# DeltaNet recurrence and SwiGLU FFN in one kernel: products of the preparation placed in the same TensorE visits as the recurrence's

## The chip, the cores and the metric

The kernel runs on one core of one Trainium2 chip. The metric is device time of one execution in microseconds (us), as the median of repeated runs. TensorE does the matrix products, VectorE and ScalarE the elementwise work, GpSimd a few small operations, and SyncE (SP in the profile) issues nearly all transfers.

## The reference

Attention of the DeltaNet kind over 4 batches, 8 heads, 768 positions and a head size of 48, and then a feed-forward block over the 3072 tokens (model size 384, inner size 1536). Everything is float32.

```python
k_n = k / (np.linalg.norm(k, axis=-1, keepdims=True) + 1e-06)
state = np.zeros((B, H, D, D))
for t in range(S):
    kt, vt, bt = k_n[:, :, t], v[:, :, t], beta[:, :, t, None]
    y[:, :, t] = np.einsum('bhd,bhde->bhe', q[:, :, t], state)
    v_old = np.einsum('bhde,bhd->bhe', state, kt)
    state = state + bt[:, :, :, None] * np.einsum('bhd,bhe->bhde', kt, vt - v_old)
x = y.transpose(0, 2, 1, 3).reshape(B * S, H * D)
g = x @ w_gate
out = (g * (1 / (1 + np.exp(-g))) * (x @ w_val)) @ w_out
```

## The kernel before

**Chunks.** The sequence is cut into 12 chunks of 64 positions. Inside a chunk the recurrence is turned into matrix products; between chunks only `state` is handed on. Chunk c's attention ends in x, and the FFN of chunk c works on it (256 tokens). While TensorE works on the FFN of chunk c, the small products of the attention of chunk c + 1 are put between its large ones. The order of the instructions of all engines is written out by hand: what the Python code issues first stands first in its engine's queue (`manual_schedule`).

**The FFN of a chunk** is six calls of `gate_val` (lines 840 to 868) and one output. Each `gate_val` makes a group of six matmuls for `p_gate` and six for `p_val`; the page counts two records to a matmul, so such a group is "x12". ScalarE takes silu into `sil` (one buffer), VectorE multiplies into `h_f`. From chunk 3 on the output is `output_fast` (line 950): seven products of six matmuls each (`p_o`, line 959, "x84" in all), with sums of `h_f` on VectorE beforehand (lines 942 to 948) and additions into `o_sb` (line 969) as products end.

**The attention of a chunk** on TensorE is made of batches of 32 products of 64x64 tiles, for which the text uses short names:

- R (`p_r`, line 742): K times state; VectorE scales `vin` by the norms (line 401) and subtracts R from it (line 759)
- Y1 (`p_y`, line 751): Q times state
- U (`p_u`, line 763): the inverse `zt` times `vin`; ScalarE copies it to `uu`
- S (`p_s`, line 794): K transposed times `uu`; VectorE adds it to `state` (line 803)
- Y2 (`p_y`, line 782): the masked K Q^T times `uu`, accumulated on Y1; ScalarE copies the sum to `y`
- F (`p_f`, line 827): six full transposes of `y`; ScalarE copies them to `x_ffn`, which the next FFN reads

They are the steps of the generator `advance` (line 730): R and Y1, then U, then S and Y2, then F.

**The preparation** that comes ahead of a chunk's attention:

- K and Q are transposed in blocks by VectorE out of `qpad` (line 422, 128x1024 each, in `turned`), which then starts the load of the next blocks on SP (line 154, eight transfers for K and eight for Q)
- K K^T (`gram`, line 444, copied to `a_sb` by line 467) and K Q^T (line 444, masked into `p_sb` by VectorE, line 459); both are batches of 32 products of 64x64 tiles
- for each pair of chunks, an inverse on VectorE (`invert`, line 641): transposes of `a_sb` into `mb` (lines 477, 480), GpSimd's power (line 655), scaling, 31 steps of two operations each (`substitute`, lines 510 and 516), and transposes into `zt` and `z1`. Its pieces are issued by `fill(n)`, which `gate_val` and the output call between their own work
- for each pair of chunks, two joins, J1 (line 706) and J2 (line 720), each 64 products of 32x32 tiles: J1 reads `a_sb` and `zt`, ScalarE scales the result to `t2`, J2 multiplies by `z1`, and ScalarE and then VectorE copy the result into `zt`

**PSUM.** The eight banks are split by hand: a pair `px`, a pair `py`, and four banks that the FFN's tiles take in turn. R, U, S, K K^T and J1 use `px`; Y1 with Y2, F, K Q^T and J2 use `py`. A pair is taken again only when its last reader is done.

**Where small products stand.** `point(c)` is called ahead of every `gate_val` and between output products. Each call issues one step of `advance(c)` if one has begun, else one piece of preparation (`prep_step`: a join, the second half of K and Q products that have been transposed, or new transposes). A stretch of small products between two large groups is called a visit here.

Of the kernel before, what the change touches and what calls it, by code (L numbers as in the profile page):

```python
# [11 lines left out]
ALU = mybir.AluOpType  # L12
# [9 lines left out]
def kernel(  # L22
# [25 lines left out]
    nc = tc.nc  # L48
# [21 lines left out]
    def ps_pair(name, tag):  # L70

        return psum.tile([128, 2, 512], FP32, name=name, tag=tag, bufs=1)

    def ps_ffn(shape, name):
        return psum.tile(shape, FP32, name=name, tag="ffn", bufs=4)
# [261 lines left out]
    def every():  # L337
        for bp in range(NB):
            for j in range(NJ):
                for n, (par, b) in enumerate(ORDER):  # L340
                    yield bp, j, par, b, bp == 0 and j == 0
# [128 lines left out]
    def gram(*args):  # L470
        for _ in gram_steps(*args):
            pass
# [100 lines left out]
    def recur(p, m=D):  # L573
        p = p[:, :, 0 : NB * NJ * m]
        return p.rearrange("p x (bp j d) -> p x bp j d", bp=NB, j=NJ)
# [120 lines left out]
    def join(g):  # L696

        zt, a, z1 = ztp[g % ZB], a_sb[g], z1s[g]
        M = HH // 2
        p_j = ps_pair("p_j", "px")[:, 0].rearrange("p (c m i) -> p c m i", c=2, m=M)  # L700
        for c in range(2):
            for m in range(M):
                for e in range(2):
                    for s in range(2):
                        dst, lo = QUADS[2 * s + e][0], QUADS[2 * s + 1][0]
                        nc.tensor.matmul(
                            p_j[dst, c, m],
                            a[lo, c, 2 * m + e, 0:R],
                            zt[lo, c, 2 * m + e, R:C],
                        )  # L710
        t2 = work.tile([128, 2, M, R], FP32, name="t2", tag="tmp", bufs=1)
        nc.scalar.mul(t2, p_j, -1.0)
        yield
        p_j = ps_pair("p_j", "py").rearrange("p e (c m i) -> p e c m i", c=2, m=M)
        for c in range(2):
            for m in range(M):
                for e in range(2):
                    for s in range(2):
                        row, hi = QUADS[2 * s + e][0], QUADS[2 * s][0]
                        nc.tensor.matmul(p_j[hi, e, c, m], z1[row, c, m], t2[row, c, m])  # L720
        zt_v = zt.rearrange("p c (m e) i -> p e c m i", e=2)
        for s, copy in ((0, nc.scalar.copy), (1, nc.vector.tensor_copy)):
            hi = QUADS[2 * s][0]
            copy(
                zt_v[hi, :, :, :, R:C].rearrange("p e c m i -> p e (c m) i"),
                p_j[hi].rearrange("p e c m i -> p e (c m) i"),
            )
        yield

    def advance(c):  # L730

        kn = knp[slot(c)]
        zt = ztp[c // 2 % ZB][:, c % 2]
        zt = zt.rearrange("p (par bp j) i -> p par bp j i", par=2, bp=NB)
        if c > 0:
            scale_v(c)
        r = vin.pop(c)
        p_y = recur(ps_pair("p_y", "py"))
        if c > 0:
            p_r = recur(ps_pair("p_r", "px"))  # L740
            for bp, j, par, b, first in every():
                nc.tensor.matmul(  # L742
                    p_r[half_of(b ^ par), par, bp, j],
                    kt[c][half_of(par), bp, j, b],
                    state[half_of(par), b, bp, j],
                    start=first,
                    stop=True,
                    skip_group_check=True,
                )
            for bp, j, par, b, first in every():  # L750
                nc.tensor.matmul(  # L751
                    p_y[half_of(b ^ par), par, bp, j],
                    qt[c][half_of(par), bp, j, b],
                    state[half_of(par), b, bp, j],
                    start=first,
                    stop=False,
                    skip_group_check=True,
                )
            nc.vector.tensor_tensor(out=r, in0=r, in1=p_r, op=ALU.subtract)  # L759
        yield  # L760
        p_u = recur(ps_pair("p_u", "px"))
        for bp, j, par, b, first in every():
            nc.tensor.matmul(  # L763
                p_u[half_of(b), par, bp, j],
                zt[half_of(b ^ par), par, bp, j],
                r[half_of(b ^ par), par, bp, j],
                start=first,
                stop=True,
                skip_group_check=True,
            )  # L770
        uu = work.tile([128, 2, NB, NJ, D], FP32, name="uu", tag="r", bufs=2)
        each = range(NB) if c == 0 else (slice(0, NB),)
        for bp in each:
            nc.scalar.copy(uu[:, :, bp], p_u[:, :, bp])
        if c + 2 < NCH:
            load_v(c + 2)
        yield
        pq = p_sb.pop(c)

        def p_of_u():  # L780
            for bp, j, par, b, first in every():
                nc.tensor.matmul(  # L782
                    p_y[half_of(b ^ par), par, bp, j],
                    pq[half_of(b), par, bp, j],
                    uu[half_of(b), par, bp, j],
                    start=(c == 0 and first),
                    stop=True,
                    skip_group_check=True,
                )

        def of_state():
            p_s = recur(ps_pair("p_s", "px"))
            for bp, j, par, b, first in every():
                nc.tensor.matmul(  # L794
                    p_s[half_of(par), b, bp, j],
                    kn[half_of(b), bp, 2 * j + par],
                    uu[half_of(b), par, bp, j],
                    start=first,
                    stop=True,
                    skip_group_check=True,  # L800
                )
            if c > 0:
                nc.vector.tensor_tensor(out=state, in0=state, in1=p_s, op=ALU.add)
            else:
                nc.scalar.copy(state, p_s)
            for later in range(AHEAD, NCH):
                if freed_by_k(later) == c:
                    load_k(later)

        if 0 < c < NCH - 1:  # L810
            of_state()
        p_of_u()
        y = work.tile([128, NB, NJ, 2, D], FP32, name="y", tag="r", bufs=2)
        for bp in each:
            nc.scalar.copy(y[:, bp, :, 0], p_y[:, 0, bp])
            for b in range(2):
                nc.scalar.copy(y[half_of(b), bp, :, 1], p_y[half_of(1 - b), 1, bp])
        yield

        y_f = y.rearrange("p bp j par d -> p bp (j par d)")  # L820
        xts[c] = ffn_pool.tile([128, KT, TOK], FP32, name="x_ffn")
        p_f = ps_pair("p_f", "py")[:, :, 0 : KT * 128]
        p_f = p_f.rearrange("p bp (t n) -> p t bp n", t=KT)
        for bp in range(NB):
            for t in range(KT):
                at = slice(t * 128, (t + 1) * 128)
                nc.tensor.transpose(p_f[:, t, bp], y_f[:, bp, at], ident)
        x_v = xts[c].rearrange("p t (bp n) -> p t bp n", bp=NB)
        for bp in each:
            nc.scalar.copy(x_v[:, :, bp], p_f[:, :, bp])  # L830
        yield
        if c == 0:
            of_state()
            yield
# [181 lines left out]
    def step(kind, fn, *args):  # L1016
        key = (kind, args or (1,))
        if key not in gens:
            gens[key] = [fn(*args), 0]
        next(gens[key][0], None)  # L1020
        gens[key][1] += 1

    def steps(kind, *args):
        return gens.get((kind, args), (None, 0))[1]

    fills = []
# [32 lines left out]
    def may_advance(c):  # L1059
        g = c // 2  # L1060
        due = {0: 1, 1: 2 + 2 * (c % 2)}.get(g, 2)
        return steps("advance", c) > 0 or (c in p_sb and steps("join", g) >= due)

    def prep_step(c):
# [23 lines left out]
        going.append(gen)  # L1088
        return True

    def point(c):

        mine = c < NCH and steps("advance", c) < 4 and may_advance(c)
        if mine and steps("advance", c) > 0:
            step("advance", advance, c)
        elif not prep_step(c - 1) and mine:
            step("advance", advance, c)

    def finish(c):

        if c < NCH:
            while not may_advance(c):
                fill_some(1000)
                prep_step(c - 1)
            while steps("advance", c) < 4:
                step("advance", advance, c)
# [190 lines left out]
```

## Time and profile before

| | |
|---|---|
| median of 8 runs | 738.26 us (738.1 to 739.06) |
| the profiled execution, its own time | 738.1 us |
| its span in the trace | 736.4 us |
| TensorE busy | 697.9 us, 95% of the span |
| TensorE weight loads, beside the products | 605.5 us |
| VectorE busy | 473.0 us, 64% |
| ScalarE, GpSimd busy | 154.6 us, 67.1 us |

Busy time is the time in which an engine had an instruction at work. The FFN of chunk 3 begins at 250.4 us after the span's start, that of chunk 4 at 306.4, of chunk 5 at 361.4, of chunk 6 at 417.5, and the last product ends at about 732 us. In the lines of the timeline the first number is the start in us from the span's start, the second the duration in us; a number in brackets is the idle time ahead of it and what ended it. Lines of the waits give the total in us, how often, and the longest.

### The profile page before, as it was taken

Reading aid. Unit: us, or ns where it says so; the run is one execution under the profiler, and the core shown is the slowest. Engines: PE = TensorE matmul, PEld = TensorE weight load, DVE = VectorE, ACT = ScalarE, POOL = GpSimd, SP = SyncE. Lnnn points to the kernel's source line nnn. Section 1 sums busy time; section 2 is a strip of 40 time slices with the busy share of each in tenths; the row PEclk is TensorE's granted clock in tenths of the full one; section 3 lists DMA queues with packets and bytes.
Section 4 is the critical chain, followed back from the end, with each engine's and each line's share of the span. In section 5 each row is a group of like instructions: output and inputs, shape, how many; then the busy total and the mean of one; then the engine's idle time right before and its main releaser. Section 6 shows DMA issues by size and latency. Waiting matters only on the chain.

```text
span 736.4 us, 22478 instructions
## 1 busy us (share of the span) xinstructions
PE 697.9 (95%) x10132; PEld 605.5 (82%) x10132; DVE 473.0 (64%) x977; ACT 154.6 (21%) x287; POOL 67.1 (9%) x46
## 2 busy tenths in 40 slices
PE   4657899999999999999999999999999999999997
PEld 3545788866787788988988988988988988989987
DVE  6999988888498163678853678854678853313122
ACT  3555443302401112021012011012011012021010
POOL 7008100202100000030000030000030000000000
PEclk9556999999999999999999999999999999999999
DMA  7775444221231112331302231302211100100000
GB/s 147 178 235 148 115 110 127 42 35 24 57 45 24 23 24 45 47 64 16 50 3 46 39 68 22 50 3 42 47 25 14 31 3 3 23 3 0 22 1 21
DMA packets 130735, 37.18 MB, mean 50 GB/s; under 512 B 122864, under 2 KB 125936, under 8 KB 130640
## 3 DMA queue, kind: packets, MB, share of 16 engines
q1 hardware_dynamic: 127184, 34.01, 22.7%
q10 hardware_dynamic: 3072, 1.57, 1.0%
q8 instruction: 79, 1.29, 0.7%
q0 software_dynamic: 384, 0.17, 0.2%
q14 instruction: 16, 0.13, 0.1%
HBM read 31.01 MB, written 4.72 MB: 49 GB/s over the span
## 4 chain that ended last, share of the span: by engine, by line
PE 80%; DVE 16%; issue 1%; POOL 1%; DMA 1%; ACT 0%; ACTq 0%; DVEq 0%; SPq 0%
PE p_gate L847 23%; PE p_val L847 23%; PE p_o L959 15%; PE p_o L876 6%; DVE tmp L510 3%; DVE zb L516 3%; PE p_g L444 2%; PE p_u L763 2%; PE p_r L742 1%; PE p_s L794 1%; PE p_y L782 1%; PE p_y L751 1%; POOL n_t L365 1%; DVE h_f L917 1%; DVE last_h L287 1%
## 5 line engine op out<-in xcount | busy, mean ns | idle before, releaser
L847 PE MATMUL p_gate<-x_ffn,wg_sb 128*128 128x256 f32 x864 | 204.9, 387 | 1.4 <-ACT x_ffn L830 1.4
L847 PE MATMUL p_val<-x_ffn,wv_sb 128*128 128x256 f32 x864 | 198.6, 380 | 0.0
L847 PEld LDWEIGHTS p_val<-x_ffn,wv_sb 128*128 128x128 f32 x864 | 164.1, 190 | 22.0
L847 PEld LDWEIGHTS p_gate<-x_ffn,wg_sb 128*128 128x128 f32 x864 | 161.6, 192 | 24.1 <-ACT x_ffn L830 1.9
L862 DVE TENSOR_TENSOR h_f<-sil,p_val 128x512 f32<-128x512 f32 x71 | 48.5, 683 | 147.5 <-PE p_val L847 147.1
L856 ACT ACTIVATE sil<-p_gate 128x512 f32<-128x512 f32 x72 | 43.0, 598 | 277.1 <-PE p_gate L847 249.4
L655 POOL TENSOR_TENSOR n_b<-mb,half 128x32 f32<-128x32 f32 x5 | 43.3, 8661 | 408.0 <-DVE mb L480 368.2
L959 PE MATMUL p_o<-wo_sb,h_f 128*128 128x192 f32 x432 | 75.6, 329 | 0.1
L959 PEld LDWEIGHTS p_o<-wo_sb,h_f 128*128 128x128 f32 x432 | 70.3, 190 | 1.2 <-DVE o_sb L969 0.7
L510 DVE TENSOR_TENSOR tmp<-zb,mb 128x31 f32<-128x31 f32 (+15 forms) x186 | 63.3, 340 | 12.1 <-PE p_j L630 6.8
L516 DVE TENSOR_TENSOR zb<-zb,tmp 128x31 f32<-128x31 f32 (+15 forms) x186 | 63.8, 343 | 6.6 <-DVE tmp L510 0.2
L969 DVE TENSOR_TENSOR o_sb<-o_sb,p_o 128x192 f32<-128x192 f32 x45 | 15.8, 350 | 53.4 <-PE p_o L959 36.2
L876 PE MATMUL p_o<-wo_sb,h_f 128*128 128x384 f32 x136 | 45.7, 490 | 0.0
L876 PEld LDWEIGHTS p_o<-wo_sb,h_f 128*128 128x128 f32 x136 | 25.4, 190 | 16.4
L959 PE MATMUL p_o<-last_k,h_f 128*128 128x192 f32 x180 | 32.2, 326 | 0.0
L959 PEld LDWEIGHTS p_o<-last_k,h_f 128*128 128x128 f32 x180 | 29.8, 190 | 0.0
L917 DVE TENSOR_TENSOR h_f<-h_f,h_f 128x256 f32<-128x256 f32 x54 | 22.4, 424 | 8.0 <-PE p_o L959 7.1
L959 PE MATMUL p_o<-last_h,h_f 128*128 128x192 f32 x144 | 26.3, 326 | 0.0
L959 PEld LDWEIGHTS p_o<-last_h,h_f 128*128 128x128 f32 x144 | 23.9, 190 | 0.0
L254 ACT ACTIVATE last_h<-last_h,rebias 128x512 int32<-128x512 uint32 (+2 forms) x26 | 15.3, 616 | 30.4 <-DVE last_h L246 30.4
L763 PEld LDWEIGHTS p_u<-vin,zt 64*64 64x64 f32 x768 | 13.7, 141 | 6.9 <-issue 3.2
L763 PE MATMUL p_u<-vin,zt 64*64 64x48 f32 x768 | 15.7, 228 | 2.4 <-DVE vin L759 1.2
(180 smaller groups left out, 691.6 us busy)
## 6 DMA issues: line engine op xcount, KB each, us to landing
vin<-in_v_dram SPq DMA_DIRECT2D x96, 48.0 KB
kn<-in_k_dram SPq DMA_DIRECT2D x40, 96.0 KB
out_dram<-o_sb SPq DMA_DIRECT2D x36, 96.0 KB
zt<-in_moe_w_out_dram SPq DMA_DIRECT2D x6, 384.0 KB
staged<-in_moe_w_out_dram SPq DMA_DIRECT2D x6, 384.0 KB
qpad<-in_q_dram SPq DMA_DIRECT2D x36, 64.0 KB
wo_sb<-in_moe_w_gate_dram SPq DMA_DIRECT2D x4, 512.0 KB
wo_sb<-in_moe_w_val_dram SPq DMA_DIRECT2D x4, 512.0 KB
```

The costliest lines, as they stand in the source:

```text
L254: nc.scalar.activation(power.bitcast(I32), power, ACTF.Relu, bias=rebias, scale=8.0)
L510: nc.vector.tensor_tensor(out=t_v, in0=zb[:, 0 : j + 1, j : j + 1].to_broadcast([128, j + 1, m]), in1=mb[:, j : j + 1, j + 1 : R].to_broad ...
L516: nc.vector.tensor_tensor(out=zb[:, 0 : j + 1, j + 1 : R], in0=zb[:, 0 : j + 1, j + 1 : R], in1=t_v, op=ALU.add,)
L655: nc.gpsimd.tensor_tensor(out=n, in0=mb.rearrange("p j i -> p (j i)")[:, 0 : R * R : R + 1], in1=half, op=ALU.pow,)
L763: nc.tensor.matmul(p_u[half_of(b), par, bp, j], zt[half_of(b ^ par), par, bp, j], r[half_of(b ^ par), par, bp, j], start=first, stop=True, ...
L847: nc.tensor.matmul(ps[name][:, i], w_sb[:, t, (f + i) * 128 : (f + i + 1) * 128], xts[c][:, t], start=(t == 0), stop=(t == KT - 1),)
L856: nc.scalar.activation(sil, ps[name], ACTF.Silu)
L862: nc.vector.tensor_tensor(out=hs[c, f], in0=sil, in1=ps["p_val"], op=ALU.mult)
L876: nc.tensor.matmul(p_o, hs[c, f - f % 2][:, f % 2, bp * 128 : (bp + 1) * 128], wo_sb[:, f], start=(f == 0), stop=(f == FT - 1),)
L917: nc.vector.tensor_tensor(out=out, in0=a, in1=b, op=ALU.subtract)
L959: nc.tensor.matmul(p[x, part], a(f - f % 2)[:, f % 2], b(f), start=not begun and f == 0, stop=f == FH - 1, skip_group_check=True,)
L969: nc.vector.tensor_tensor(out=out, in0=a, in1=b, op=ALU.add)
```

## The change

`advance` is cut anew for every chunk: R and its subtraction are a step, and Y1 goes to U's step. From the FFN of chunk 3 on (c > 3), `point` calls a new function `merged(c)`, which goes through fixed stages: 0, K's and Q's transposes on VectorE at the chunk's start; 1, R with K Q^T and, for even c, J1 (not until the pair's inverse has been issued); 2, J2 for even c, with K K^T of a later chunk; 3, Y1 with U; 4, S with Y2; 5, F. K Q^T moves from the chunk before to the chunk that uses it, K K^T from about the end of one FFN to the second or third visit of the next. The first join takes one of the FFN's four banks instead of `px`.

The order of TensorE's instructions, by FFN; g is a group of gate, v of val, o the output's products (o18 is 18 matmuls), square brackets are visits. J1, J2 in the FFN of chunk 2 before belong to the join of the first form.

```
FFN  before
 2   g v [J2] g v g v [KK+KQ] g v [R+Y1] g v [U] g v [S+Y2] o [F] o [J1]
 3   g v [J2] g v g v [KQ] g v [R+Y1] g v [U] g v [S+Y2] o18 [F] o24 [KK+KQ]
 4   g v [R+Y1] g v [U] g v [S+Y2] g v [F] g v g v [KK+KQ] o42      (6 the same)
 5   g v g v [J1] g v [J2] g v [R+Y1] g v [U] g v [S+Y2] o18 [F] o24 [KK+KQ]   (7 the same)
 8   g v [R+Y1] g v [U] g v [S+Y2] g v [F] g v g v [KQ] o42
 9   as 5, with [KQ] at the end
10   g v [R+Y1] g v [U] g v [Y2] g v [F] g v g v o42
FFN  after
 2   g v [J2] g v g v [KK+KQ] g v [R] g v [Y1+U] g v [S+Y2] o [F] o
 3   g v [R+KQ+J1] g v [J2] g v [Y1+U] g v [S+Y2] g v [F] g v o42
 4   g v [R+KQ] g v [KK] g v [Y1+U] g v [S+Y2] g v [F] g v o42      (6, 8 the same)
 5   g v g v g v g v [R+KQ+J1] g v [J2+KK] g v [Y1+U] o18 [S+Y2] o12 [F] o12   (7 the same)
 9   as 5, with [J2] alone
10   g v [R+KQ] g v [Y1+U] g v [Y2] g v [F] g v g v o42
```

The diff:

```diff
@@ join
-        p_j = ps_pair("p_j", "px")[:, 0].rearrange("p (c m i) -> p c m i", c=2, m=M)
+        p_j = ps_ffn([128, 512], "p_j").rearrange("p (c m i) -> p c m i", c=2, m=M)
@@ advance
         r = vin.pop(c)
-        p_y = recur(ps_pair("p_y", "py"))
         if c > 0:
             p_r = recur(ps_pair("p_r", "px"))
             for bp, j, par, b, first in every():
...
+            nc.vector.tensor_tensor(out=r, in0=r, in1=p_r, op=ALU.subtract)
+        yield
+        p_y = recur(ps_pair("p_y", "py"))
+        if c > 0:
             for bp, j, par, b, first in every():
                 nc.tensor.matmul(
                     p_y[half_of(b ^ par), par, bp, j],
...
-            nc.vector.tensor_tensor(out=r, in0=r, in1=p_r, op=ALU.subtract)
-        yield
         p_u = recur(ps_pair("p_u", "px"))
@@ ahead of point
+    stage_of = {}
+
+    def merged(c):
+        if c >= NCH:
+            return
+        at, k_c, q_c = stage_of.get(c, (0, None, None))
+        g = c // 2
+
+        def a_step():
+            step("advance", advance, c)
+
+        def gram_k(tag):
+            if k_c is not None:
+                gram(k_c, False, tag, (nc.vector.tensor_copy,) * 2)
+                if k_c % 2 == 1:
+                    fills.append((k_c // 2, invert(k_c // 2)))
+
+        def j_step():
+            if c % 2 == 0 and steps("join", g) < 2:
+                step("join", join, g)
+
+        if at == 0:
+            if going:
+                next(going.pop())
+                return
+            if k_of and steps("advance", freed_by_k(k_of[0])) >= 4:
+                k_c = k_of.pop(0)
+                turned(k_c, False)
+            if q_of and q_of[0] == c:
+                q_c = q_of.pop(0)
+                turned(q_c, True)
+        elif at == 1:
+            if c % 2 == 0 and g not in inverted:
+                return
+            a_step()
+            if q_c is not None:
+                gram(q_c, True, "py")
+            if c % 2 == 0:
+                j_step()
+            elif k_c is None:
+                at = 2
+        elif at == 2:
+            if c % 2 == 0:
+                j_step()
+            gram_k("px")
+        elif at < 6:
+            a_step()
+        stage_of[c] = (at + 1, k_c, q_c)
+
     def point(c):
+        if c > 3:
+            merged(c)
+            return
@@ finish
-        if c < NCH:
+        if c > 3:
+            while c < NCH and steps("advance", c) < 4:
+                if stage_of.get(c, (0,))[0] == 1 and c % 2 == 0 and c // 2 not in inverted:
+                    fill_some(1000)
+                merged(c)
+        elif c < NCH:
```

## The prediction

> **What bounds the kernel now.** I read the engine shares first, then the slices with the clock row, then TensorE's waits, then its timeline.
>
> ```profile
> PE 697.9 (95%) x10132; PEld 605.5 (82%) x10132; DVE 473.0 (64%) x977; ACT 154.6 (21%) x287; POOL 67.1 (9%) x46
> PE   4657899999999999999999999999999999999997
> DVE  6999988888498163678853678854678853313122
> PEclk9556999999999999999999999999999999999999
> ```
>
> TensorE is full from the seventh slice on, at full clock, so what the change touches (FFN 3 on, from 250 us) is a TensorE queue: only shorter TensorE work or fewer TensorE waits count there. From 230 us on TensorE waits for just two things:
>
> ```profile
> PE p_g L444 <- DVE kt L422: 1.9, 2, 0.9
> PE p_g L444 <- DVE qt L422: 1.0, 1, 1.0
> ```
>
> The timeline of TensorE (start us, duration us) prices a visit of small matmuls. First stretch: FFN 5. Second: the only place where 64x64 tiles are followed at once by 32x32 ones. Third: a wait, in FFN 6.
>
> ```profile
> 382.39 2.75 PE L847 MATMUL p_val<-x_ffn,wv_sb 128*128 128x256 f32 x12
> 385.08 1.15 PE L742 MATMUL p_r<-state,kt 64*64 64x48 f32 x64
> 386.04 1.11 PE L751 MATMUL p_y<-state,qt 64*64 64x48 f32 x64
> 387.09 2.86 PE L847 MATMUL p_gate<-x_ffn,wg_sb 128*128 128x256 f32 x12
> 389.78 2.75 PE L847 MATMUL p_val<-x_ffn,wv_sb 128*128 128x256 f32 x12
> 392.46 1.15 PE L763 MATMUL p_u<-vin,zt 64*64 64x48 f32 x64
> 393.54 2.86 PE L847 MATMUL p_gate<-x_ffn,wg_sb 128*128 128x256 f32 x12
> 396.24 2.75 PE L847 MATMUL p_val<-x_ffn,wv_sb 128*128 128x256 f32 x12
> ...
> 67.49 1.15 PE L794 MATMUL p_s<-uu,kn 64*64 64x48 f32 x64
> 68.57 0.75 PE L620 MATMUL p_j<-zt,a_sb 32*32 32x32 f32 x64
> ...
> 452.41 2.75 PE L847 MATMUL p_val<-x_ffn,wv_sb 128*128 128x256 f32 x12
> 456.11 1.16 PE L444 MATMUL p_g<-kt 64*64 64x64 f32 x64 [0.95 <-DVE kt L422]
> 457.33 1.16 PE L444 MATMUL p_g<-qt,kt 64*64 64x64 f32 x64
> 458.42 2.22 PE L959 MATMUL p_o<-wo_sb,h_f 128*128 128x192 f32 x12
> ```
>
> Durations overlap, so I use start to start. Without a visit beside it, a gate or val group takes 2.59 (447.23 to 449.82). From 389.78 to 396.24 two groups and a lone U take 6.46: U costs 6.46 - 5.18 = **1.28**. From 382.39 to 389.78, with R and Y1: 7.39 - 5.18 = **2.21**. So a second product costs 0.93 and the visit itself **0.35**, as delays of about 0.10 before it, 0.12 at its end and 0.10 in the group after it. A lone join (375.80 to 379.70 and on) costs 1.41, so its product is 1.06. F, in full 128x128 tiles, leaves its neighbours at 2.59: it is no visit in this sense.
>
> The wait: val of 452.41 ends at 455.00, the next group starts at 458.42; 3.42 where two products take 2.0. VectorE's timeline shows why:
>
> ```profile
> 454.44 0.43 DVE L516 TENSOR_TENSOR zb<-zb,tmp 128x256 f32<-128x256 f32 x1
> 454.81 1.25 DVE L422 STREAM_TRANSPOSE kt<-qpad 128x1024 f32<-128x1024 f32 x1
> 455.98 1.20 DVE L422 STREAM_TRANSPOSE qt<-qpad 128x1024 f32<-128x1024 f32 x1
> ```
>
> The transposes of K and Q stand behind substitution steps of the inverse, and TensorE is asked for K K^T immediately after them.
>
> [...] S to J1 above takes 1.08 where S to Y2 takes 0.96 (398.92 to 399.89), so 0.12 is seen. [...]
>
> **The change, part by part.** The orders of instructions say what moves; the number of matmuls does not change.
>
> *Visits.* From FFN 2 on there are 45 visits before and 36 after (F left out): FFN 2 six to five; FFN 3, 5, 7 and 9 six to four; FFN 4, 6 and 8 four and four; FFN 10 three and three. By chunk, with the products that come or go: FFN 2 loses J1 as a visit of its own, -1.41; FFN 3 loses two visits, K K^T and one K Q^T and gains J1, -0.70 - 1.86 + 1.06 = -1.50; FFN 5, 7 and 9 lose two visits each, -0.70; FFN 8 gains K K^T, +0.93; FFN 10 gains K Q^T, +0.93. Together **-3.15**, which is nine visits at 0.35.
> Against it stand six changes of mode inside visits: J1 behind K Q^T in FFN 3, 5, 7, 9, and K K^T behind J2 in FFN 5 and 7. Each is at least the 0.12 seen and at most 0.22 (0.12 and another 0.10, as a group after a visit shows). I take 0.17: **+1.0**. Ends: 0.7 to 1.3, and 0 if nothing of it adds.
>
> *The waits that go.* By the prices, FFN 4 would take 6 x 5.18 + 3 x 2.21 + 1.28 + 0.65 (F) + 13.65 (42 output matmuls) = 53.3; it takes 306.41 to 361.44 = 55.0. FFN 6: 417.46 to 472.48, the same. FFN 8 (K Q^T alone: 52.4) takes 528.50 to 582.08 = 53.6. The differences are 1.7, 1.7 and 1.2: **-4.6**. They are VectorE's lateness at K K^T, and 0.2 more at the last output product in FFN 4 and 6. After, both transposes are issued at the chunk's start, when VectorE has only the last o_sb add before them: they run from 0.5 to 2.9 us, and K Q^T is asked for at 6.2. That cover is 3.3 us; K K^T comes 7 us later still.
>
> *The wait that is new.* R's subtract, K Q^T's mask and the inverse now meet in FFN 5, 7 and 9. Every step, with row durations: K K^T in FFN 4 is at 12.6 to 13.7 us. VectorE: copies to a_sb to 15.1; three transposes of 2.14 and one product to 22.1; GpSimd's power 6.2 to 28.4 (POOL n_b, L655); norms, beta and scaling of mb, 3.57 as at 432.43 to 436.00, to 32.1 (behind h_f and its sums). 31 steps of two operations follow, 0.45 to 0.92 each, 23.3 together; 15 are done when FFN 4 ends. In FFN 5, from its start: 0.5 (last o_sb add), seven steps 6.3, the transposes of K and Q 2.3, two steps 1.6, h_f 0.6, five steps 3.3, h_f 0.6, two steps 1.0: 16.1. Then zt's transposes 5.8 as at 365.47 to 371.27: **21.8**. J1 stands behind R and K Q^T, four pairs in: 20.7 + 2.0 = 22.7, so 0.9 to spare. Then h_f 0.6, z1 2.4, h_f with sums 1.9, vin scaling 1.05, subtract 0.9, mask 1.25: **29.8**. Bank pair py is held by K Q^T until then, and J2 writes py: it is asked for at 20.7 + 3.4 + 5.2 = 29.4. With the handover of 0.1, TensorE waits **0.5**; FFN 7 is the same. In FFN 9 there is no K to transpose, all is 1.2 earlier, no wait. Sum **+1.0**; ends 0 and 4 (each sum of some 40 durations may be off by 1.5). What is queued behind J2 is all of TensorE.
>
> *Costed at nothing.* Y1 moves to U's visit: its products are in the sum; py is taken later, and U's operand vin is ready then, since a group lies between R and it. (At 89.37 U waited 1.22 for vin; VectorE sets that time, with Y1 before it or not.) The first join's bank in the four-bank FFN ring: v3 must be freed before gate 5; h_f frees it at 22.4, gate 5 starts at 24.1: 1.7 to spare, and if that cover goes, each us late is a us. ScalarE (21%) keeps all its copies; F follows Y2 by 3.9 us of output products where y's three copies take 1.44, and x_ffn's 0.8 has 3.9 behind F. SP: the sixteen loads of K and Q blocks (4 to 6 us of issue for each eight) go behind the output's four instead of ahead of them; they land for a transpose some 50 us later, where the shortest interval before was 43. v's and kn's loads move with U and S by up to 10 us, for a use over 50 us on. GpSimd: the same seven operations a pair of chunks, alone.
>
> **Sum.** 738.1 (profiled; its span is 736.4 and 1.7 lies around it; the median is 738.26, 0.02% off) - 3.15 + 1.0 - 4.6 + 1.0 = **732.3**.
>
> **Rivals.** (1) *The waits move along*: K Q^T now waits for qt at its new place. For: VectorE runs behind in even chunks. Against: no inverse is running at the start of FFN 4, 6 and 8. Only the visits count: 738.1 - 2.1 = 736.0.
> (2) *VectorE becomes the bound in FFN 5, 7 and 9*, and the kernel is **slower**: the inverse starts 14 us later in FFN 4 than before (K K^T was ahead of its first gate), so zt, subtract and mask come late. With an added lateness of L the waits are 2(0.5 + L) + (L - 0.8). They eat the 6.75 of gains at L = 2.2, and cost over 0.2% from L = 2.7. At L = 4 the time is 743.5. Before, FFN 5 shows VectorE just as late: h_f at 371.27 belongs to a val that ended 5 us earlier. Against: my sum leaves 0.5.
> (3) *Between them*, L = 1 to 1.5: 735.3.
> (4) *It does not merge*: the order shows that it does; nothing is left for this.
>
> **Numbers.** Chances: forecast 0.70, (1) 0.09, (3) 0.08, L around 2.2 and so no change 0.06, (2) 0.07. About 0.2% (1.5 us) can be told from no change. Some of (1) falls within it: faster 0.83, same 0.09, slower 0.08. Range: 738.1 - 3.15 - 4.6 = 730.3 with no new cost; upward to (1) and (3), 736.3.
>
> **What would show it.** FFN 4, 6 and 8 at 53.3 us each with no wait at L444; FFN 5 and 7 near 56.2; the transposes of K and Q within 3 us of the chunk's start; zt's end at 21.8 and the mask's at 29.8 in FFN 5; a wait of some 0.5 us of J2 for p_sb. Wrong: waits of over 2 us at J1 or J2 (rival 2), a wait of K Q^T for qt (rival 1), or visits that cost as much when merged.

## The result, and the profile after

The kernel after the change takes **742.27 us** as a median of 11 runs (741.76 to 747.15), the one before 738.65 us in 31 runs taken with it: ratio 1.0065, 95% interval 1.0055 to 1.0076. It is slower, where 732.3 us and faster was forecast. The profiled execution of after takes 746.21 us, with a span of 744.5, so it is one of the longer ones; the section on the prediction says how the two stand to each other.

The engine shares and the clock row of the page of after, to be laid beside those of before:

```profile
PE 702.8 (94%) x10132; PEld 611.1 (82%) x10132; DVE 472.4 (63%) x977; ACT 154.4 (21%) x287; POOL 64.1 (9%) x46
...
PEclk9556999999999999999999999999999999999999
```

The number of TensorE records is the same, but they take 702.8 us in place of 697.9, and more idle time lies between them. The clock row shows nothing of it: a loss of 3 us does not show in a slice of 18.6. TensorE's waits from 230 us on name it (total, times, longest, in us):

```profile
PE p_j L706 <- issue: 5.4, 4, 1.6
```

No wait for kt or qt is left, and none of J2 for `p_sb`. In their place the first join stands still four times, with nothing in another engine that it waits for ("issue"). TensorE's timeline in FFN 3, at the merged visit:

```profile
256.10 1.15 PE L741 MATMUL p_r<-state,kt 64*64 64x48 f32 x64
257.06 1.13 PE L444 MATMUL p_g<-qt,kt 64*64 64x64 f32 x64
258.12 0.87 PE L706 MATMUL p_j<-zt,a_sb 32*32 32x32 f32 x79
260.27 0.62 PE L706 MATMUL p_j<-zt,a_sb 32*32 32x32 f32 x49 [1.28 <-issue]
260.83 4.54 PE L848 MATMUL p_gate<-x_ffn,wg_sb 128*128 128x256 f32 x12
265.21 2.75 PE L848 MATMUL p_val<-x_ffn,wv_sb 128*128 128x256 f32 x12
```

The idle time falls inside J1, after 79 of its 128 records, where no operand changes. Then the gate group takes 4.38 us from start to start where it took 2.69. The windows of the same stretch (from:to, length, busy time of PE, PEld, DVE, ACT and POOL with the number of records, granted clock, DMA share, GB/s) say why:

```profile
255.50:259.00 3.50, 3.49 (x211) 2.95 (x209) 2.69 (x3) 0.00 (x0) 0.00 (x0) 1.00 0.02 5
259.00:260.50 1.50, 0.23 (x27) 0.23 (x31) 1.49 (x2) 0.00 (x0) 0.00 (x0) 1.00 0.00 0
...
261.50:264.00 2.50, 2.50 (x7) 1.96 (x7) 1.25 (x3) 0.04 (x1) 0.00 (x0) 0.50 0.00 0
```

TensorE is full, then empty for 1.3 us, then runs at half the clock (granted 0.50). The transfers hint at what it ran out of. This is the DMA view from 256 to 262 us (40 slices of 0.15 us; then queue, packets, MB, share), with all that moved in those 6 us:

```profile
DMA  0000000000003000000000000000000000030000
...
q8 instruction: 2, 0.03, 1.9%
```

Two packets, both of instructions; the first starts at 257.9 and ends at 258.75, and J1 goes on 1.5 us later. The page has the queue's total:

```profile
q8 instruction: 79, 1.29, 0.7%
```

1.29 MB in 79 packets is 16 KB each. TensorE's 2 x 10132 records over 79 are 256.5 for a packet. So if the packets of this queue bring TensorE's instructions, one brings some 256 of them; that is an estimate from these numbers, and the counts of records in all traces, further down, fit it. The visit of FFN 3 is 512 records, matmuls and weight loads together (128 each for R and K Q^T, 256 for J1), as many as two such packets would hold. Its first 414 pass in 2.9 us; then TensorE stands.

The other three J1s do the same: idle 1.41, 1.57 and 1.15 us, after 112, 24 and 64 of their 128 matmul records.

### The profile page after: what moved, and what is told of

Read it like the earlier page. It is cut to its first block, busy times and chain, and to the rows that moved or that the text cites. A ratio compares the mean times of both kernels' runs of the same rounds, so it can differ in the third digit from the quotient of the medians.

```text
span 744.5 us, 22474 instructions
## 1 busy us (share of the span) xinstructions
PE 702.8 (94%) x10132; PEld 611.1 (82%) x10132; DVE 472.4 (63%) x977; ACT 154.4 (21%) x287; POOL 64.1 (9%) x46
## 3 DMA queue, kind: packets, MB, share of 16 engines
q10 hardware_dynamic: 3072, 1.57, 1.0%
q8 instruction: 79, 1.29, 0.7%
## 4 chain that ended last, share of the span: by engine, by line
PE 89%; DVE 6%; issue 2%; ACT 1%; DMA 1%; SPq 0%; ACTq 0%; DVEq 0%
PE p_gate L848 27%; PE p_val L848 25%; PE p_o L960 17%; PE p_o L877 6%; PE p_g L444 2%; PE p_y L783 2%; PE p_u L764 2%; PE p_s L795 2%; DVE zb L516 1%; DVE tmp L510 1%; PE p_r L741 1%; PE p_y L754 1%; PE p_f L828 1%; PE p_j L630 1%; PE p_j L706 1%
## 5 line engine op out<-in xcount | busy, mean ns | idle before, releaser
L848 PE MATMUL p_gate<-x_ffn,wg_sb 128*128 128x256 f32 x864 | 211.1, 396 | 1.3 <-ACT x_ffn L831 1.3
L848 PEld LDWEIGHTS p_gate<-x_ffn,wg_sb 128*128 128x128 f32 x864 | 166.9, 198 | 25.9 <-ACT x_ffn L831 1.8
L655 POOL TENSOR_TENSOR n_b<-mb,half 128x32 f32<-128x32 f32 x5 | 41.0, 8194 | 427.9 <-DVE mb L480 386.3
L775 ACT COPY uu<-p_u 128x768 f32<-128x768 f32 (+1 forms) x13 | 9.6, 748 | 40.4 <-PE p_u L764 40.4
```

The source lines that it names most:

```text
L655: nc.gpsimd.tensor_tensor(out=n, in0=mb.rearrange("p j i -> p (j i)")[:, 0 : R * R : R + 1], in1=half, op=ALU.pow,)
L848: nc.tensor.matmul(ps[name][:, i], w_sb[:, t, (f + i) * 128 : (f + i + 1) * 128], xts[c][:, t], start=(t == 0), stop=(t == KT - 1),)
```

## The experiments

Three theories were set against each other. **F**: the visit of 512 records uses its instructions faster than they are brought. **M**: the change of tile size inside a visit is far dearer than taken. **B**: the FFN's bank, which the first join now uses, is what costs. Later runs set F against **P**: it depends only on where the blocks of 256 happen to end. Beside each measured time stands its ratio to before.

**1. J1 apart.** J1 keeps its new bank but stands between a gate and a val group.

```diff
             elif at == 1: ...
                 if c % 2 == 0:
-                    j_step()
+                    later_join.append(j_step)
...
             if name == "p_gate": ...
+                while later_join:
+                    later_join.pop()()
```

> The changed kernel, except that the first join J1 leaves the visit of R and K Q^T: in the FFN of chunks 3, 5, 7 and 9 it stands between the gate and the val group that follow, so one visit of 512 TensorE instructions (a record of a matmul and one of its weight load each count as one) becomes two of 256. Everything else, J1's bank in the FFN ring included, stays. Theory F (feeding): TensorE's instructions come by transfer in blocks of 16 KB, 256 instructions, and a visit that uses up a whole block in less than about 2.9 us runs dry. F expects no idle inside J1, the clock at 1.00 through all four chunks, and visits at their old prices: the forecast of 732.3 with one visit more and one change of mode less in four chunks, 4 x (0.35 - 0.17) = 0.7, so 733.0. Theory B (J1's new bank makes it wait): idle at J1 stays and the time stays near 742. Theory M (the third change of the tiling mode in one visit is what costs): also a gain, to about 733; the next kernel tells M from F.

Measured: 737.78 us, ratio 0.9987 (0.9977 to 0.9996). No J1 stands still, and FFN 3, 5 and 9 take 54.86, 56.11 and 54.86 us in place of 57.84, 58.94 and 57.71. So the bank as such costs nothing. But F's 733.0 is missed, most of it in FFN 7, which takes 60.19: there the visit of J2 and K K^T, 384 records and J1's 256 some 5 us ahead of them, runs dry (timeline). The 2.9 us that F allows a block in its expectation is an estimate, and no trace shows it as a limit; in FFN 7 of after J1 goes on at 499.02 us, 2.89 after the start of its packet (496.13).

```profile
502.51 1.16 PE L444 MATMUL p_g<-kt 64*64 64x64 f32 x64 [2.18 <-issue]
503.61 4.54 PE L849 MATMUL p_gate<-x_ffn,wg_sb 128*128 128x256 f32 x12
```

**2. The kernel before, with J1's products issued twice.** 512 records of one tile size and in the old bank, nothing else changed; the work added is 64 products in each of four joins.

```diff
-        for c in range(2):
+        for c in (0, 1, 0, 1):
```

> The kernel before, with the 64 products of J1 issued twice in J1's own visit (the same results written twice), in the FFN of chunks 3, 5, 7 and 9: 512 instructions of one tiling mode, with J1's old bank and nothing merged. F expects idle inside J1 of 1.3 to 1.8 us in each, at a place that has to do with the block's end, and, if the clock follows the idle, half clock for 3.4 us after it: per chunk 1.06 for the products, some 1.5 of idle and up to 1.7 for the clock, so +10 to +17 on 738.6: 749 to 755. M and B expect no idle: 4 x 1.06 = 4.2 more, 742.8.

Measured: 760.87 us, ratio 1.0296 (1.0273 to 1.0319), above every figure expected. Without a change of tile and without the new bank TensorE stands still in all four, here in the one at the end of FFN 2 (it is of line 706 like the others; only the J2 of FFN 2 belongs to the join of the first form):

```profile
249.31 2.46 PE L706 MATMUL p_j<-zt,a_sb 32*32 32x32 f32 x231
254.01 0.39 PE L706 MATMUL p_j<-zt,a_sb 32*32 32x32 f32 x25 [2.24 <-issue]
```

M and B fall as the cause. The profiled execution is 24.1 us above before's; the added products are 4 x 1.06 of it, so a dense visit loses some 5 us on average: 2.2 to 2.4 idle, the rest slower work behind it, as at half clock: the gate group after J1 takes 4.38, 3.78, 5.28 and 5.21 us from start to start where before's takes 2.69. The expectation took the idle time too small, and its 1.7 for the clock was passed in two of the four.

**3. J1 apart, and K Q^T issued three times in FFN 4, 6, 8 and 10.** 512 records again, now of 64x64 tiles, which take longer each: is it the number of records that decides?

```diff
-        for bp, j, par, b, _ in every():
+        again = 3 if of_q and c > 4 and c % 2 == 1 else 1
+        for bp, j, par, b, _ in list(every()) * again:
```

> The first kernel of this call, with the 32 products of K Q^T issued three times in the visit of R in the FFN of chunks 4, 6, 8 and 10 (same results): 512 instructions again, but of 64x64 tiles only, which use a block of 256 in 1.9 us instead of 1.1. F expects idle of about 2.9 - 1.9 = 1.0 us in each of the four visits; with the products' 4 x 1.86 that is +11.4 on the first kernel (about 744.5), and more where the clock drops. M and B expect the products alone, +7.4 (about 740.5), without idle.

Measured: 749.53 us, ratio 1.0145 (1.0131 to 1.0159): 11.75 above experiment 1, where F had 11.4 and the others 7.4. Three of the four visits run dry, by 1.43, 1.63 and 0.79 us; the one in FFN 6 does not. The first:

```profile
316.55 0.68 PE L445 MATMUL p_g<-qt,kt 64*64 64x64 f32 x28 [1.43 <-issue]
```

The total fits F, but one in four got through (the count of instructions below shows why), and in these three no half clock followed (the gate group behind takes its 2.69 us). The agreement of the sum is thus better than that of its parts.

**4. The kernel after, with 128 records more early on** (K Q^T of chunk 1 issued twice), which shifts where the blocks end. A single run.

```diff
-        for bp, j, par, b, _ in every():
+        again = 2 if of_q and c == 1 else 1
+        for bp, j, par, b, _ in list(every()) * again:
```

> The changed kernel with the 32 products of K Q^T of chunk 1 issued twice, early in the FFN of chunk 0 (same results): all later TensorE instructions move by 128 against the blocks of 256, that is by 64 of the records that the timeline counts. In the changed kernel J1's idle begins after 79, 112, 24 and 64 of its 128 records in the FFN of chunks 3, 5, 7, 9. F expects the idle at 15, 48, about 88 and 0 (or the end of K Q^T). M, B and anything else that belongs to J1 itself expect the old places. Time: that of the changed kernel, plus 0 to 1 us.

Measured: 744.99 us, above the 742.3 to 743.3 expected, but within the range of after's own runs. In FFN 5 and 7 the idle time moved to J1's records 48 and 88, both as expected; the first:

```profile
386.82 0.89 PE L707 MATMUL p_j<-zt,a_sb 32*32 32x32 f32 x80 [1.63 <-issue]
```

In FFN 3 it came in J2 instead, after 118 records, and in FFN 9 behind J1, at the gate; and K K^T stood still in FFN 5 and 7 as well (1.55 and 1.43). Two places of four came as expected. The place moved with the count of instructions and not with the operands; why FFN 3 and 9 differ is shown below.

**5. All visits at 256 records at most.** Experiment 1, and K K^T of FFN 5 and 7 also between the next gate and val.

```diff
             elif at == 2: ...
-                gram_k("px")
+                later_join.append(lambda: gram_k("px"))
```

> The first kernel (J1 apart), with K K^T also taken out of J2's visit in the FFN of chunks 5 and 7: J2 stays where it is and K K^T stands between the next gate and val group. No visit from the FFN of chunk 3 on has over 256 TensorE instructions. F expects no idle for which the profile shows no reason from there on, the clock at 1.00, and two more visits at 0.35 less two changes of mode at 0.17, +0.4 on the forecast of 733.0: 733.4 plus what the start of the execution varies by (in the profiled executions so far the FFN of chunk 3 starts 0 to 2.5 us later than the sum says), so 733.4 to 736, and a ratio near 0.994. M expects nothing gained over the first kernel, about 738.

Measured: 738.04 us, ratio 0.9988 (0.9978 to 0.9999); a miss. FFN 5 takes 56.29, but FFN 7 takes 60.97. Its timeline, and the DMA view from 488 to 504 us (slices of 0.4 us):

```profile
497.51 1.28 PE L720 MATMUL p_j<-t,z 32*32 32x32 f32 x128 [0.39 <-DVE p_sb L459]
501.52 4.44 PE L849 MATMUL p_gate<-x_ffn,wg_sb 128*128 128x256 f32 x12 [2.73 <-issue]
```

```profile
DMA  0010000000010000000000000001000000001000
```

Packets start at 489.1, 492.7, 499.2 and 502.7. The second ends at 494.0, and in the 5.2 us from there to the third nothing at all is transferred, so the third was not held up by other traffic. So visits of 256 close behind one another can run dry as well (J1 and J2 start 4.46 us apart here, and 2.73 us are lost). In FFN 7 of experiments 1, 3 and 5 a wait of J2 for `p_sb` (0.2 to 0.4 us) stood ahead of the idle time, and in FFN 5, where nothing ran dry in them, there was none. But such a wait isn't needed: in FFN 3 of experiment 4 J2 ran dry behind a packet as late, with no wait ahead of it. Why the packet comes late in these places stays open.

**6. The kernel after, unaltered, in another profiled execution**, for how much of this repeats.

> The changed kernel once more, unaltered: are idle and half clock always the same? F expects idle of 1.1 to 1.6 us inside J1 at the same records (79, 112, 24, 64 of 128), as the blocks of instructions lie where they lay. [...] it follows in some of the four only, and the time is lower than the profiled 746.2 by 1.7 us for each that is missing; if it is a fixed part of the visit, it comes all four times and the time is 746 again.

Measured: 747.27 us. The four J1s stand still after the same records as in the first profile, for 1.28, 1.96, 0.77 and 1.73 us, and J2 in FFN 7 in addition (1.83). For the half clock two cases were set side by side: it follows in some of the four only, with 1.7 us less for each that is missing, or all four times with 746 again. It follows three of the five stretches (1.28, 1.96 and 1.73; the gate group behind takes 4.38, 4.05 and 4.39 us from start to start, 2.69 after the other two), but the time isn't lower, since the idle time is 7.6 us in place of 5.4. The places of J1 came again; the lengths, and whether half clock follows, differ between the two executions.

**7. The kernel before, with the transposes of K and Q one point earlier in FFN 4, 6 and 8.** This asks whether the waits that the prediction counted as gone need no more than an earlier place.

```diff
             step("advance", advance, c)
+            if c > 4 and c % 2 == 1 and steps("advance", c) == 4:
+                prep_step(c - 1)
```

> The kernel before with one thing alone: in the FFN of chunks 4, 6 and 8 the VectorE transposes of K and Q are issued with F instead of one point later, so that K K^T and K Q^T stand a pair of gate and val groups after them. Visits, joins, R with Y1 and the banks stay as before. By the forecast's second term the wait of TensorE for VectorE (1.7, 1.7 and 1.2 us) goes: 738.6 - 4.6 = 734.0, ratio 0.994. If that wait only moves on (the copies of K K^T and the mask stand behind the inverse too, and the output's sums behind them), the time stays at 738.

Measured: 740.26 us, ratio 1.0022 (1.0015 to 1.003), slower. The wait moves to the output (FFN 4; 1.84 and 0.64 in FFN 6 and 8):

```profile
352.27 0.92 PE L959 MATMUL p_o<-last_k,h_f 128*128 128x192 f32 x4 [1.85 <-DVE h_f L917]
```

VectorE was not late with one operation; it had too much to do ahead of FFN 4's end. The change relieves it there by starting the inverse later: 25 of its 31 steps fall into FFN 4 before, 15 after. VectorE's busy time within FFN 4 (third pair of numbers), before and then after:

```profile
306.41:361.44 55.03, 53.98 (x690) 48.42 (x684) 45.51 (x94) 7.24 (x13) 7.34 (x3) 1.00 0.31 48
```

```profile
308.66:361.97 53.31, 53.31 (x683) 48.22 (x683) 36.19 (x72) 7.24 (x13) 6.58 (x3) 1.00 0.24 39
```

**8. Both joins apart, and K K^T of FFN 5 and 7 behind F.** No visit above 256 records, one gate group between R with K Q^T and J1, and two groups, val and gate, between the joins; the rest as after the change.

```diff
             elif at == 1: ...
                 if c % 2 == 0:
-                    j_step()
+                    later_join.append(j_step)
             elif at == 2:
                 if c % 2 == 0:
-                    j_step()
-                gram_k("px")
+                    later_join.append(j_step)
+                else:
+                    gram_k("px")
             elif at < 6:
                 a_step()
+                if at == 5 and c % 2 == 0:
+                    gram_k("px")
```

> The edit: in the merged kernel both joins stand between a gate and a val group (J1 as in the earlier run with J1 apart, J2 one group later), and K K^T of FFN 5 and 7 goes behind F in the output. No visit holds more than 256 TensorE instructions, and in the dense stretch from [R+KQ] to the end of [Y1+U] there are some 840 instructions in 17.8 us, 5.4 us for each 256, where the run with K K^T apart had 256 in 3.2 us and ran dry in FFN 7. Theory F (TensorE runs out of instructions where 256 of them take less time than their transfers are apart, 3.3 us and more): no idle time put down to issue of over 0.5 us from FFN 3 on, no half clock, FFN 5 and 7 at 56 to 57 us each. The sum: J1 apart measured 737.8 with 4.1 us lost in FFN 7, so 733.7, and two visits more at 0.35 less two changes of mode of 0.17: 734.1; with a wait of U for zt, which J2 now leaves only a val group to copy, of 0 to 0.5 in each of four chunks: 734 to 736. Rival P (what runs dry depends on where the 256-instruction blocks happen to end, whatever the visits): idle of 1 to 3 us and a half clock in one or two chunks again, 736.5 to 739.

Measured: **733.79 us**, ratio 0.9934 (0.9922 to 0.9947), against 734.1 of the sum: faster than before and than after. From 230 us on the view of waits lists none for TensorE, and the clock stays full. FFN 3 (timeline):

```profile
257.87 2.86 PE L849 MATMUL p_gate<-x_ffn,wg_sb 128*128 128x256 f32 x12
260.65 1.29 PE L706 MATMUL p_j<-zt,a_sb 32*32 32x32 f32 x128
261.87 2.42 PE L849 MATMUL p_val<-x_ffn,wv_sb 128*128 128x256 f32 x10
```

J1's 128 records run through without a stop. Keep dense visits apart and the loss is gone; P alone, which had idle time again and 736.5 to 739, falls. The margin is thin in FFN 7: J2 takes 1.55 us there instead of 1.29, since it pauses for 0.24 us, too short for the view of waits, until 1.44 us after the end of a packet. This kernel removed the wait of J2 in FFN 7 together with the density, so it doesn't tell those two apart.

**Where the idle time begins and ends, over all runs.** In the traces of after (both) and of experiments 1 to 5 there are 25 idle stretches of over 0.5 us put down to issue from 230 us on. Every one ends 1.2 to 1.55 us after the end of a 16 KB instruction packet, and 2.2 to 2.9 us after its start:

```
kernel, place             TensorE idle      packet            resumes after its end
after, FFN 3, J1          258.99-260.27     257.86-258.75     1.52
after, FFN 5, J1          385.96-387.37     385.19-386.17     1.20
after, FFN 7, J1          497.45-499.02     496.13-497.50     1.52
experiment 1, FFN 7, KK   500.33-502.51     500.19-501.27     1.24
experiment 2, FFN 9, J1   611.56-613.99     611.77-612.73     1.26
experiment 5, FFN 7, gate 498.79-501.52     499.15-500.09     1.43
```

The packet before it began 5 to 26 us earlier (19.7 in FFN 3 of after), while elsewhere packets follow one another in as little as 3.3 us. So it is not the queue's rate that is exhausted, as the expectations had it. The reading that fits, an inference, is that the 2.2 to 2.9 us from a packet's start to the resumption are longer than what TensorE still has in hand lasts.

The traces also give the place to the instruction. All records of TensorE are counted from the start of the span: matmuls, weight loads, and the 77 to 92 of its sequencer (semaphores and drains). Before every one of the 25 resumptions the count is a multiple of 256 plus 193:

```
after, both executions   7873, 11201, 14273, 17601; in the second also 14785
experiment 1             14785
experiment 2             7873, 11457, 15041, 18369
experiment 3             9665, 15297, 16577, 19905
experiment 4             8385, 11201, 11713, 14529, 15041, 17857
experiment 5             14785
```

So wherever TensorE stops in these traces, it is at the same place of a count by 256, whatever the operands, tile and bank. Beside packets of 16 KB for 256.5 records each this is read here as the end of a block; no trace shows which instructions a packet holds. Read so, in all ten traces no packet starts while TensorE has more than 298 records left up to the first that the packet brings, so that what it has in hand would be little more than one block.

This tells which visits are hit. In the 20 visits of 512 (after twice, experiments 2, 3 and 4) a block ends at record 304 or later in 18. Its packet starts 0.9 to 2.9 us after the visit has begun, and all 18 run dry at that record. In the other two, FFN 6 of experiment 3 and FFN 3 of experiment 4, the last block ends at records 281 and 286; its packet had started 1.6 and 1.2 us ahead of the visit, and both got through. So P has a part in it: a dense visit is hit here when a block ends late enough inside it. K K^T of experiment 4 is hit in the same way, at records 302 and 382 of 384. In the five stretches left (J2 or what follows it in FFN 7 of experiments 1, 3, 5 and 6, and in FFN 3 of experiment 4) the block ended at record 236 to 256 of the visit, but the packet was late: it started 4.5 to 6.4 us after TensorE had come within 307 records of it, and 1.0 to 1.9 us in the 20 others.

## Why the prediction was wrong, and where it was right

By FFN, in us against before. The second column is the prediction's own terms put to the FFN that they belong to; the others are distances from the first gate of one FFN to that of the next in the profiled executions, less those of before.

```
FFN              2      3      4      5      6      7      8      9     10     sum
forecast      -1.41  -1.33  -1.70  +0.14  -1.70  +0.14  -0.27  -0.53  +0.93   -5.73
after         -1.33  +1.84  -1.72  +2.92  -1.71  +3.13  -0.26  +2.62  +0.85   +6.34
experiment 8  -1.32  -1.15  -1.71  +0.12  -1.70  +0.38  -0.26  -0.23  +0.84   -5.03
```

**The step that failed** is *Visits*: the merged visit of R, K Q^T and J1 was costed at its products, one visit, and a change of mode (of tile size). Each of the four took 2.8 to 3.2 us more, 12.1 together. The supply of TensorE's instructions has no term in the sum. By the traces 5.4 of the 12.1 is TensorE idle with nothing in another engine to wait for, and the 6.7 left is mostly the four gate groups behind, at half clock: 4.38, 4.16, 4.33 and 4.38 us from start to start where they took 2.69. 732.3 and 12.1, and 1.7 for a later start of FFN 2 in that execution (193.24 against 191.5), for which the prediction has no term either, together give 746.1; 746.21 was profiled. The median is 4 us lower. Experiment 6 shows that idle time without half clock occurs; that this is what sets the median apart from the profiled execution is an inference. The mean granted clocks on record fit it: 0.956 in the profiled execution, 0.965 to 0.975 in the six runs near the median, 0.959 in the slowest.

No rival named this. The sign of rival 2 was right by accident: VectorE is not the bound. Its times in FFN 5, which begins at 361.97 after the change (timeline of VectorE; `zt`'s last transposes, then the mask):

```profile
379.64 3.92 DVE L480 STREAM_TRANSPOSE zt<-zb 32x1024 f32<-32x1024 f32 x2
...
390.35 1.28 DVE L459 TENSOR_TENSOR p_sb<-p_g,mask_q 128x512 f32<-128x512 f32 x2
```

The transposes end 21.6 us after the start where 21.8 was worked out, and the mask 29.7 where it was 29.8. Long sums of durations on one engine held to 0.2 us.

**Point by point.**
- *FFN 4, 6 and 8 at 53.3*: 53.31, 53.31 and 53.32. The waits at line 444 are gone, as forecast. The reason given was half of it: experiment 7 shows that an earlier place of the transposes alone only passes the wait on to the output. That the inverse's later start frees VectorE is read from its steps and busy time, and was not tested apart.
- *A visit costs 0.35*: FFN 2, which loses one visit and has no dense one, came out at -1.33 for -1.41. In experiment 8 the prices of the visits left give every FFN to 0.12 us, but for FFN 7, which takes 0.38 more than before where they say 0. The runs show the price, not its cause.
- *Changes of mode at 0.17*: smaller where the tile size changes from 64x64 to 32x32. In FFN 3 J1 starts 1.06 us after K Q^T, which starts 0.96 after R: 0.10 for the change, just under the lower end of 0.12. For K K^T behind J2, from 32x32 to 64x64, the price was an estimate alone.
- *J2's wait of 0.5 in FFN 5 and 7*: not seen after the change, since TensorE was itself late; 0.24 and 0.39 in FFN 7 of experiments 1 and 5, none in FFN 5.
- *"Visits that cost as much when merged"* was on the list of what would make the prediction wrong. They cost more.

The profile of before held the hint: 79 instruction packets of 16 KB beside 10132 records of matmuls and as many of weight loads, a join of 256 records in 1.3 us, and from FFN 2 on no visit of more than 256. The queue's share of 0.7% says nothing here; the question was how soon the next packet could be there, and the working did not ask it.

## What to carry to other kernels

A batch of small matmuls is cheap by its durations, and joining batches saves the price of a visit (0.35 us here), but instructions have to be brought too: count the records between two large groups and set them against the blocks in which they seem to arrive (some 256 records in a packet of 16 KB here). Spread dense batches among operations that last long per instruction. Here one gate group (24 records in 2.6 us) between R with K Q^T and J1 was enough in experiments 1, 5 and 8; between the two joins one was too little in FFN 7 (experiment 5), and two were just enough (experiment 8). Where a block ends can hide the loss or bring it out, so a change of some instructions elsewhere can move it, as experiment 4 did. A short idle time on TensorE may be paid twice, as in FFN 3 of after, where 1.28 us of it were followed by a gate group of 4.38 us in place of 2.69, so look for "issue" in the waits and at the clock in windows of a few us, since the page's 40 slices hide both.

## What the runs showed of the hardware that was not expected

- In all 25 idle stretches TensorE goes on 1.2 to 1.55 us after the end of an instruction packet of 16 KB, whose transfer takes 0.9 to 1.6 us (before and after, from 230 us on), and the profile names nothing else that it waits for.
- In the profiled execution of after, half clock (granted 0.50) comes from 230 us on in four stretches of 3.41 us, which begin at 261.04, 387.33, 499.97 and 612.61 us, from 0.04 us before TensorE goes on to 1.18 after. In the traces of before and after all changes of the granted clock lie whole multiples of 3.413 us apart (the four starts 37, 33 and 33 of them). By the durations of the products behind the 25 idle stretches, TensorE slowed down after all 8 of 1.96 us or more (2.73 was the most), after none of the 3 under 0.8, and after 6 of the 14 between 1.15 and 1.88. Length alone doesn't decide there: in experiment 6, 1.83 us cost no clock and 1.28 did. What decides stays open.
- FFN 2 begins at 191.5 to 192.1 us in the three kernels with before's order there, and at 192.05 to 193.93 in the seven other executions. In the FFN of chunks 0 and 1 the change splits R from Y1 as it does later; whether that or something else makes the difference was not looked for.
